# Order of the far stretches in the weighted value sums of a sliding-window attention kernel

## The chip, the core and the metric

The kernel runs on one core of a Trainium2 chip. A core has a matrix engine (TensorE, PE in the profile, with its weight loads shown apart as PEld), a vector engine (DVE), a scalar engine (ACT), GpSimd (POOL), a queue engine (SP) and 16 DMA engines. The metric is the device time of one execution in microseconds. Before the change the median of three runs is 258.38 us (258.15 to 258.97).

## The reference

The input is 2048 tokens of 512 channels. They are normalised, and the output is the sum of the input and of two branches.

- Branch A is attention with 32 heads of 16 channels. A token looks at itself and the 255 tokens before it. `qkv = xn @ wqkv`, `p = softmax(q k^T / 4)` inside the window, `o = p v`, and `o @ wo`.
- Branch B is a gated mixer: `z = gelu(xn @ w_in)` with 1376 channels; the second half is normalised and mixed over tokens by a full 2048 x 2048 matrix, a bias for each token is added, the product with the first half goes through `w_out`.

What the change touches is `o = p v` of branch A: for each block of queries, the sum of the value rows of at most 511 keys, weighted by the exponentials of the scores, and the sum of these weights.

## The kernel before

All work is in one program whose order is written out by hand in three strings of tokens, STAGE1, STAGE2 and STAGE3; each token is a call (the dictionary `ops`). An engine executes its instructions in the order of the tokens. STAGE1 computes branch B up to the gelu and the first projections; STAGE2 mixes tokens of branch B (`H`, line 553, matmuls of 344 columns), projects queries, keys and values (`Q`, `K`, `P`), and does the attention; STAGE3 ends with the last output projections. The tokens of attention lie between those of the mixing, so that TensorE has other work while the scalar engine takes exponentials.

Heads are taken in 4 groups G of 8. For one group:

- `S` (line 431) computes scores: keys on 128 partitions, queries along the columns, 8 heads, into the four banks of `sS`. `X` (line 445) takes the exponentials into `E`, a ring of 2560 columns for each of 8 heads. For a block of 128 keys, `kb`, `E` holds 320 columns of queries: partitions 0 to 63 hold the near keys, 64 to 127 the far ones, and the query columns of the two halves are shifted by 64, which is why a key block needs 320 columns and not 384. `M` multiplies the edges of the window by masks.
- `V` (`visit`, line 500) computes the value sums. There are 8 blocks u of 256 queries in a head group. For each, the sum runs over key blocks `2u-2` to `2u+1`, in two halves: half 0 (here called near) takes keys 0 to 63 of each key block, half 1 (far) takes keys 64 to 127. So a near matmul uses the rows 0 to 63 of the array, a far one rows 64 to 127. A weight load brings 64 keys x 17 columns of `v_all` (16 value channels and a column of ones, which makes the sum of the weights).
- A call `V,i` does the near half of block i and the far half of block i-1, one beside the other: the two write different banks (`oP`, two of them). The far half of block i-1 finishes that block, and `N` on the vector engine then reads the bank, divides, and transposes.

One stretch is a run of query columns that belongs to one key block and one half of the heads (`e`, 0 or 1). It is done by four pairs of weight load and matmul, one for each of 4 heads, in four strips of 32 output partitions (`32 * s`). A half of a full block has 8 stretches, two each of 64, 128, 192 and 256 columns, 1280 columns in all. A block at the start of a head group (u = 0) has only two key blocks: 4 stretches, of 128 and 256 columns in the near half and of 192 and 64 in the far half.

`av_half` (line 467) lists the stretches of one half in `todo`, sorts them by length, and yields each with `at`, the number of columns that this half has done before it. The near half goes from short to long, except for block u = 1, the far half from long to short. `visit` merges the two lists by `at`, so that the order of instructions follows the two halves as if each moved one column at the same time; with equal `at` the near one comes first. `V,32`, the last call, has a far half alone.

Of the kernel before, what the change touches and what calls it, by code (L numbers as in the profile page):

```python
# [31 lines left out]
BAND = 320  # L32
WARM = 29
NCEN = 3


def kb_start(kb):
    return BAND * kb if kb < NB - 1 else BAND * (NB - 2) + 256


def kb_len(kb):
    return min(BAND, S_TOK - kb * P)
# [135 lines left out]
def kernel(  # L178
# [69 lines left out]
    xs = s1.tile([P, NB, D], BF, name="xs")  # L248
    xc = s1.tile([P, NCEN, D], BF, name="xc")
    xcT = s1.tile([P, NCEN, NDC, P], BF, name="xcT")  # L250

# [30 lines left out]
    def x_transpose(n, bank):  # L282
        xn = xc[:, n, :] if n < NCEN else xs[:, n, :]
        tp = banks[bank].bitcast(BF)[:, 0:512].rearrange("p (c q) -> p c q", c=NDC)
        for c in range(NDC):
            nc.tensor.transpose(out=tp[:, c, :], in_=xn[:, c * P : (c + 1) * P], identity=ident[:])  # L286

    def x_copy(n, bank, eng):
        tp = banks[bank].bitcast(BF)[:, 0:512].rearrange("p (c q) -> p c q", c=NDC)
        if n < NCEN:  # L290
            for c in (0, 2):
# [14 lines left out]
    def gate(n, half, tag, p0, p1):  # L306
        zp = zrot[tag]
        f0 = half * FH
        for c in range(2 * p0, 2 * p1):
            for lo, hi in Z_RANGES:  # L310
                nc.tensor.matmul(  # L311
                    zp[:, lo:hi],
                    lhsT=xcT[:, n, c, :] if n < NCEN else xnT[:, c, n * P : (n + 1) * P],
                    rhs=w_in_sb[:, c, f0 + lo : f0 + hi],
# [4 lines left out]
    def gelu(n, half, tag):  # L319
        zp = zrot[tag]  # L320
        dst = z1u[:, n + 1, 0:FH] if half == 0 else z2[:, n, :]

        scale = rstdx[:, n : n + 1] if n < NCEN else 1.0
        nc.scalar.activation(out=dst, in_=zp[:, 0:FH], func=ACT.Gelu_apprx_tanh, scale=scale)  # L324
# [142 lines left out]
    def av_half(G, u, half):  # L467

        a = 2 * u
        r0 = 64 * half
        bank = oP[(G * 8 + u) % 2]
        todo = []
        for kb in range(max(0, a - 2), a + 2):

            lo = max(0, a * P - kb * P - r0)
            hi = min(kb_len(kb) - (r0 if kb >= NB - 2 else 0), (a + 2) * P - kb * P - r0)
            assert lo < hi, (u, half, kb)
            todo += [(hi - lo, kb, lo, hi, e) for e in range(2)]  # L480

        up = half == 0 and (G * 8 + u) % 8 != 1
        todo.sort(key=lambda t: (t[0] if up else -t[0], t[1], t[4]))
        at = 0
        for i, (n, kb, lo, hi, e) in enumerate(todo):
            o0 = e * 256 + kb * P + lo + r0 - a * P
            col = (kb_start(kb) + lo) % RING
            yield at, [
                dict(
                    out=bank[32 * s : 32 * s + DH + 1, o0 : o0 + n],  # L490
                    lhsT=v_all[r0 : r0 + 64, kb, HG * G + 4 * e + s, :],
                    rhs=E[r0 : r0 + 64, 4 * e + s, col : col + n],
                    start=(half == 0 and i == 0),
                    stop=(half == 1 and i == len(todo) - 1),
                )
                for s in range(4)
            ]
            at += n

    def visit(i):  # L500

        top = list(av_half(i // 8, i % 8, 0)) if i < NG * 8 else []
        low = list(av_half((i - 1) // 8, (i - 1) % 8, 1)) if i >= 1 else []
        if not top:

            nc.tensor.matmul(
                oP[i % 2][0 : DH + 1, 0:1], lhsT=v_all[0:64, 0, 0, :], rhs=E[0:64, 0, 0:1],
                start=True, stop=True, skip_group_check=True,
            )
        for _, four in sorted(top + low, key=lambda t: t[0]):  # L510
            for args in four:
                nc.tensor.matmul(skip_group_check=True, **args)  # L512
# [263 lines left out]
```

## Time and profile before

| | us |
|---|---|
| median of three runs | 258.38 |
| the profiled execution | 258.61 |
| its span, first to last instruction | 256.9 |
| around the span | 1.71 |
| TensorE busy | 248.8 |
| DVE busy | 186.2 |
| ACT busy | 181.0 |
| matmuls of the visits, line 512, busy | 24.8 |

The page gives each engine's busy time, a chain of the work that ended last, and groups of instructions by line with "busy, mean ns of one, idle before". A shape such as 64*17 64x256 says: 64 rows and 17 columns of weights, 256 columns of data. Matmuls overlap in the pipeline, and the profile's duration of one is its latency; how fast they follow one another is seen by counting starts in short windows. A row of such windows reads: window, its length, busy time of PE with the count of matmuls in it, busy time of PEld with the count of weight loads, the granted TensorE clock, the DMA share and GB/s. Windows that begin together and end later and later give running counts. The timeline merges neighbours of one kind: start, length, engine, line, names, shape of the first, count. The granted clock is 1.000 throughout.

### The profile page before, as it was taken

How to read it: one execution, taken by the hardware profiler on the slowest of the kernel's cores; microseconds unless marked ns; L12 is line 12 of the kernel's file. 1: busy time of each engine (PE TensorE's matmuls, PEld its weight loads, DVE VectorE, ACT ScalarE, POOL GpSimd, SP SyncE). 2: the span in 40 equal slices, each digit the busy share in tenths (PEclk: the TensorE clock that was granted, in tenths of full speed). 3: DMA queues.
4: the chain of work that ended last, by engine and by line, in shares of the span. 5: the costliest groups of instructions: out<-in, count | busy, mean ns of one | idle time of the engine just before them, and what ended most of it. 6: DMA issues, size and time to landing. Idle time of an engine off the chain costs nothing.

```text
span 256.9 us, 9051 instructions
## 1 busy us (share of the span) xinstructions
PE 248.8 (97%) x3900; PEld 139.3 (54%) x3936; DVE 186.2 (72%) x412; ACT 181.0 (70%) x142; POOL 92.0 (36%) x172
## 2 busy tenths in 40 slices
PE   7999999999999999999999999999999999999995
PEld 6565555433456555655555655655555544444454
DVE  4887877888797676768775767758877487666764
ACT  3686566899978687777778776867687787777400
POOL 7514110430016176017288053603645343611110
PEclk9999999999999999999999999999999999999999
DMA  7985743269404886659969549998775632644432
GB/s 233 362 242 103 124 82 81 72 134 220 100 3 86 111 148 137 116 110 133 145 125 166 115 83 113 128 148 146 140 144 114 125 74 84 115 123 119 115 98 68
DMA packets 69945, 32.67 MB, mean 127 GB/s; under 512 B 60833, under 2 KB 66945, under 8 KB 69905
## 3 DMA queue, kind: packets, MB, share of 16 engines
q1 hardware_dynamic: 64000, 20.79, 44.1%
q0 software_dynamic: 4672, 9.97, 17.6%
q10 hardware_dynamic: 1232, 1.32, 1.5%
q8 instruction: 31, 0.51, 0.9%
q14 instruction: 10, 0.07, 0.1%
HBM read 8.41 MB, written 2.10 MB: 41 GB/s over the span
## 4 chain that ended last, share of the span: by engine, by line
PE 93%; ACT 3%; issue 1%; DMA 1%; DVE 1%
PE w L553 31%; PE sS L431 10%; PE w L341 10%; PE oP L512 8%; PE w L583 6%; PE zb L311 5%; PE za L311 5%; PE zo L311 5%; PE w L396 4%; PE w L589 4%; ACT E L445 2%; DMA xs<-in_A_x_dram 1%; PE w L286 1%; PE w L605 1%; PE tj L583 1%
## 5 line engine op out<-in xcount | busy, mean ns | idle before, releaser
L445 ACT ACTIVATE E<-sS 128x2048 bf16<-128x2048 f32 x76 | 142.6, 1877 | 41.9 <-PE sS L431 40.8
L553 PE MATMUL w<-z,wspT 128*128 128x344 bf16 x512 | 92.6, 310 | 0.7 <-issue 0.2
L553 PEld LDWEIGHTS <-wspT 128*128 128x128 bf16 x512 | 46.9, 98 | 31.5 <-issue 5.9
L389 POOL DMA_DIRECT2D kbd<-kz x48 | 29.5, 623 | 60.4 <-DVE kz L381 58.3
L368 POOL DMA_DIRECT2D q<-qs x54 | 28.0, 529 | 29.2 <-DVE qs L357 22.0
L454 DVE TENSOR_TENSOR E<-E,mask 128x1024 bf16<-128x1024 bf16 x52 | 34.7, 675 | 4.3 <-ACT E L445 4.3
L341 PE MATMUL w<-xnT,wqkv 128*128 128x512 bf16 x106 | 35.7, 380 | 0.7 <-issue 0.3
L431 PE MATMUL sS<-q,kbd 32*128 32x320 bf16 (+4 forms) x816 | 30.4, 244 | 0.3
L560 DVE SCALAR_TENSOR_TENSOR z1u<-w,b_all,z1u 128x344 bf16<-128x344 f32 x32 | 18.2, 568 | 16.4 <-PE w L553 16.3
L520 DVE STREAM_TRANSPOSE a<-oP 128x512 f32<-128x512 f32 x32 | 22.7, 709 | 5.4 <-PE oP L512 5.3
L512 PE MATMUL oP<-E,v_all 64*17 64x256 bf16 (+3 forms) x1920 | 24.8, 230 | 0.4 <-issue 0.4
L512 PEld LDWEIGHTS <-v_all 64*17 64x17 bf16 x1920 | 20.2, 85 | 9.0 <-issue 8.8
L311 PEld LDWEIGHTS <-xnT 128*128 128x128 bf16 x208 | 18.3, 98 | 12.4
L431 PEld LDWEIGHTS <-kbd 32*128 32x128 bf16 x816 | 12.2, 92 | 22.2 <-issue 20.0
L583 PE MATMUL w<-w_out_sb,z1u 128*128 128x512 bf16 x67 | 19.1, 380 | 0.5 <-issue 0.3
L577 POOL DMA_DIRECT2D wqkv<-in_A_x_dram x16 | 8.9, 558 | 28.3 <-DVE out_sb L597 27.5
L341 PEld LDWEIGHTS <-wqkv 128*128 128x128 bf16 x128 | 12.1, 98 | 9.6 <-issue 1.2
L329 DVE BATCH_NORM_STATS2 st<-z 128x6 f32<-128x344 bf16 x32 | 14.4, 492 | 2.6 <-ACT z L324 2.6
L396 PE MATMUL w<-wqkv,xnT 128*128 128x512 bf16 x63 | 16.2, 380 | 0.0
L533 DVE STREAM_TRANSPOSE oT<-b 128x256 bf16<-128x256 bf16 x32 | 14.2, 445 | 1.1
L381 DVE CAST kz<-w 128x256 bf16<-128x256 f32 x26 | 9.8, 418 | 6.5 <-PE w L341 4.4
L589 PE MATMUL w<-wo_sb,oT 128*128 128x512 bf16 x47 | 13.8, 380 | 0.0
(95 smaller groups left out, 248.9 us busy)
## 6 DMA issues: line engine op xcount, KB each, us to landing
kbd<-kz POOLq DMA_DIRECT2D x48, 64.0 KB, 3.3
q<-qs POOLq DMA_DIRECT2D x36, 64.0 KB, 3.8
wqkv<-in_A_x_dram POOLq DMA_DIRECT2D x16, 128.0 KB, 3.5
wqkv<-in_A_wqkv_dram SPq DMA_DIRECT2D x1, 1536.0 KB
out_dram<-out_sb SPq DMA_DIRECT2D x11, 128.0 KB, 2.7
xs<-in_A_x_dram SPq DMA_DIRECT2D x2, 512.0 KB, 7.5
kbd<-kz SPq DMA_DIRECT2D x16, 64.0 KB, 2.1
q<-qs SPq DMA_DIRECT2D x14, 64.0 KB, 2.3
```

Source lines behind the costliest of these rows:

```text
L311: nc.tensor.matmul(zp[:, lo:hi], lhsT=xcT[:, n, c, :] if n < NCEN else xnT[:, c, n * P : (n + 1) * P], rhs=w_in_sb[:, c, f0 + lo : f0 + hi ...
L341: nc.tensor.matmul(banks[bank], lhsT=wqkv[:, c, col : col + P], rhs=xnT[:, c, tok : tok + 512], start=(c == 0), stop=(c == NDC - 1),)
L368: eng.dma_start(out=q2[h : P : 2, e, c : c + w], in_=t[64 * e : 64 * e + 64, src0 + at : src0 + at + w],)
L389: eng.dma_start(out=kbd[h : P : 2, slot : slot + 4, e, :], in_=t[64 * e : 64 * e + 64, h, :].rearrange("p (k m) -> p k m", k=4),)
L396: nc.tensor.matmul(banks[bank], lhsT=xnT[:, c, n * P : (n + 1) * P], rhs=wqkv[:, c, 2 * D : 3 * D], start=(c == 0), stop=(c == NDC - 1),)
L431: nc.tensor.matmul(s_bank(s)[:, off + o : off + o + w], lhsT=kbd[32 * s : 32 * s + 32, slot, ee, :], rhs=q2[32 * s : 32 * s + 32, ee, c : ...
L445: nc.scalar.activation(out=dst, in_=src, func=ACT.Exp, scale=SM_SCALE)
L454: nc.vector.tensor_tensor(out=reg, in0=reg, in1=mask[:].rearrange("p a m -> p (a m)").unsqueeze(1).to_broadcast([P, 8, 128]), op=ALU.mult,)
L512: nc.tensor.matmul(skip_group_check=True, **args)
L553: nc.tensor.matmul(banks[bank][:, 0:FQ], lhsT=w[:, c, :], rhs=z2[:, c, half * FQ : (half + 1) * FQ], start=(c == 0), stop=(c == NB - 1),)
L583: nc.tensor.matmul(banks[bank], lhsT=uT[:, c, :], rhs=w_out_sb[:, c, :], start=(c == 0), stop=False)
L589: nc.tensor.matmul(banks[bank], lhsT=oT[:, G, n * P : (n + 1) * P], rhs=wo_sb[:, G, :], start=False, stop=(G == NG - 1),)
```

## The change

The sorted list of the far half is put in another order by a fixed permutation. With lengths, the far half of a full block before and after:

- before: 256, 256, 192, 192, 128, 128, 64, 64 columns, so that stretches begin at columns 0, 256, 512, 704, 896, 1024, 1152, 1216
- FAR, blocks u = 1 to 6: 192, 128, 128, 64, 192, 256, 256, 64 columns, beginning at 0, 192, 320, 448, 512, 704, 960, 1216
- FAR_LAST, block u = 7, which lies beside the near half of the next head group's first block: 64, 128, 128, 256, 256, 192, 192, 64 columns, beginning at 0, 64, 192, 320, 576, 832, 1024, 1216

The near half of a full block begins its stretches at 0, 64, 128, 256, 384, 576, 768, 1024, and the first block of a head group at 0, 128, 256, 512. Block u = 0 keeps its order, as do all near halves. The stretch that ends the far half is the same as before. No instruction is added or taken away.

```diff
+FAR = (2, 4, 5, 6, 3, 0, 1, 7)
+FAR_LAST = (6, 4, 5, 0, 1, 2, 3, 7)
...
         up = half == 0 and (G * 8 + u) % 8 != 1
         todo.sort(key=lambda t: (t[0] if up else -t[0], t[1], t[4]))
+        if half == 1 and u:
+            todo = [todo[k] for k in (FAR_LAST if u == 7 else FAR)]
         at = 0
```

## The prediction

> **What bounds the kernel now.** I read the page first: the share of each engine, then the chain that ended last, then the groups of the changed line.
>
> ```profile
> span 256.9 us, 9051 instructions
> ...
> PE 248.8 (97%) x3900; PEld 139.3 (54%) x3936; DVE 186.2 (72%) x412; ACT 181.0 (70%) x142; POOL 92.0 (36%) x172
> ...
> PE 93%; ACT 3%; issue 1%; DMA 1%; DVE 1%
> PE w L553 31%; PE sS L431 10%; PE w L341 10%; PE oP L512 8%; PE w L583 6%; PE zb L311 5%; PE za L311 5%; PE zo L311 5%; PE w L396 4%; PE w L589 4%; ACT E L445 2%; DMA xs<-in_A_x_dram 1%; PE w L286 1%; PE w L605 1%; PE tj L583 1%
> ...
> L445 ACT ACTIVATE E<-sS 128x2048 bf16<-128x2048 f32 x76 | 142.6, 1877 | 41.9 <-PE sS L431 40.8
> ...
> L512 PE MATMUL oP<-E,v_all 64*17 64x256 bf16 (+3 forms) x1920 | 24.8, 230 | 0.4 <-issue 0.4
> L512 PEld LDWEIGHTS <-v_all 64*17 64x17 bf16 x1920 | 20.2, 85 | 9.0 <-issue 8.8
> ```
>
> TensorE is the bound: 97% busy, 93% of the chain, and the next engine, ACT, spends 40.8 of its 41.9 us of idle time there waiting for TensorE's scores. So what a visit (line 512) gains or loses reaches the end, unless TensorE meets a wait for something else soon after. All visits together are 8% of the chain, about 20 us, in 1920 pairs of a weight load and a matmul.
>
> The page cannot say how one visit runs, and its mean of 230 ns is latency, not spacing. So the second view is one ordinary full visit, at 118.38 us, with its matmuls kept apart by shape:
>
> ```profile
> L512 PE MATMUL oP<-E,v_all 64*17 64x256 bf16 x16 | 0.7, 271 | 0.0
> L512 PE MATMUL oP<-E,v_all 64*17 64x128 bf16 x16 | 0.6, 216 | 0.0
> L512 PE MATMUL oP<-E,v_all 64*17 64x64 bf16 x16 | 0.5, 191 | 0.0
> L512 PE MATMUL oP<-E,v_all 64*17 64x192 bf16 x16 | 0.4, 243 | 0.0
> ```
>
> From 64 to 256 columns is 80 ns more, so a column costs 0.417 ns and about 164 ns are pipeline latency. Sixty-four columns occupy their strip of the array for 27 ns, 128 for 53, 192 for 80, 256 for 107; I add 2 ns for the change.
>
> The third view opens windows that all begin with this visit and end later and later, for line 512 alone. The count behind PE is how many matmuls have started by the window's end, the count behind PEld how many weight loads:
>
> ```profile
> 118.38:118.43 0.05, 0.05 (x12) 0.05 (x15) 1.00 0.86 195
> 118.38:118.50 0.12, 0.12 (x16) 0.12 (x24) 1.00 1.12 216
> 118.38:118.53 0.15, 0.15 (x24) 0.15 (x32) 1.00 1.14 232
> 118.38:118.61 0.23, 0.23 (x28) 0.23 (x33) 1.00 1.17 246
> 118.38:118.62 0.24, 0.24 (x28) 0.24 (x35) 1.00 1.16 246
> 118.38:118.64 0.26, 0.26 (x32) 0.26 (x37) 1.00 1.43 248
> 118.38:118.70 0.32, 0.32 (x36) 0.32 (x37) 1.00 1.47 246
> 118.38:118.71 0.33, 0.33 (x38) 0.33 (x38) 1.00 1.46 246
> 118.38:118.79 0.41, 0.41 (x45) 0.41 (x48) 1.00 1.44 254
> 118.38:118.84 0.46, 0.46 (x48) 0.46 (x54) 1.00 1.79 311
> 118.38:118.87 0.49, 0.49 (x56) 0.49 (x57) 1.00 1.75 303
> 118.38:118.91 0.53, 0.53 (x58) 0.53 (x62) 1.00 1.66 289
> 118.38:118.94 0.56, 0.56 (x62) 0.56 (x64) 1.00 1.62 284
> 118.38:118.95 0.57, 0.57 (x64) 0.57 (x64) 1.00 1.60 279
> ```
>
> Three things stand in it. First, 15 loads go out in 0.05 us, one pair in 3.3 ns. Second, load 33 is out by 0.23 us at the latest, and then loads stop for reasons that are not in the code: 34 and 35 come between 0.23 and 0.24 us, load 37 by 0.26, load 38 only between 0.32 and 0.33. Third, from then on they come in steps: from x38 at 0.33 to x62 at 0.53 is 24 loads in 0.20 us, 8.3 ns each, though 15 went out in 0.05 us at the start.
>
> I read this as a limit on how many instructions may be unfinished. Thirty-two pairs are 64 instructions. The 65th and 66th go, and the 67th (load 34) goes about 0.03 us after the first matmul has ended (191 ns by its row). The 75th (load 38) goes just as much after the fifth matmul has ended: that is the first of the far half, 256 columns, started at about 14 ns, so done at 14 + 271 = 285 ns, and 285 + 35 = 320. So places come free in order, a matmul holds its place until it is finished, and a freed backlog is handed on at 4.2 ns an instruction.
>
> A shorter visit, in which the far half is that of a head group's first block and has only 4 stretches (96 instructions; the near half goes from long to short there), shows no such step:
>
> ```profile
> 112.05:112.25 0.20, 0.20 (x20) 0.20 (x28) 1.00 1.25 268
> 112.05:112.37 0.32, 0.32 (x32) 0.32 (x34) 1.00 1.12 238
> 112.05:112.38 0.33, 0.33 (x32) 0.33 (x36) 1.00 1.10 233
> ```
>
> The 65th instruction is due there only after places are free again, and two still go out within 0.01 us at 0.33 us.
>
> The Trainium skill, TensorE: Matmul & The Clock Gate, opening table of specifications, gives TensorE a queue of 64 with a partial reorder window; the stop after the 65th or 66th instruction agrees. It does not say that a place is held until the matmul ends; by the queue's depth alone, with places freed at issue, no stretch would be held up and the change would bring the small gain of the first rival below, so here the rows decide.
>
> **The change, part by part.** No instruction, wait, transfer or byte is added or removed, and on DVE, ACT, POOL, SP and the DMA queues nothing moves; their cost is nothing because no step of theirs is touched. Only the order of pairs inside 27 visits changes (and in the last, which has the far half alone): 24 full visits (6 in each head group) by FAR, and 3 at the change of head group by FAR_LAST. All far operands were complete when the near half of that block was visited before, so no wait is added; the last stretch is the same, so DVE's waiting transpose is released by the same matmul.
>
> What it removes: the shared columns, at 256 and 1024. At the first, matmuls 17 to 24 start between 0.12 and 0.15 us; the far one could start at 14 + 107 + 2 = 123 ns and had, by x24 at 0.15, at most some 10 ns of delay. At the second, matmuls 49 to 56 start between 0.46 and 0.49, where near was free at 0.349 + 0.109 = 0.458 (its eleventh group began with load 41, three steps of 8.3 ns after load 38, and 4 ns). I put each at 5 ns, bounds 0 and 10: 0 to 20 ns a visit.
>
> What it adds: it moves short far stretches forward and long ones back, so other work falls on places 65 and up. Groups of four pairs (one for each strip), N near, F far, with columns: before N64 F256 N64 N128 N128 F256 N192 F192, then N192 F192 N256 F128 N256 F128 F64 F64. After: N64 F192 N64 N128 F128 N128 F128 N192, then F64 F192 N192 F256 N256 F256 N256 F64. Before, the ninth group was not due until about 0.26 and the tenth not until 0.32, when the place was free anyway. After, the far half runs at 14, 96, 151 ns and its 64 columns are due at 206 ns, the next F192 at 235 ns. In ns, first and fourth strip:
> - ninth, F64: 206, and by loads 34 to 36 at 230 and more, 247 for the fourth.
> - tenth, F192: load 37 at 253, matmul 257. The fifth matmul is now 192 columns, done 271 - 243 = 28 ns earlier, so load 38 goes at 320 - 28 = 292: strips two to four at 296, 304, 313. They were due at 240 to 270.
> - eleventh, N192, due at 259: pairs 8.3 ns apart, so 321 to 346.
> - twelfth, F256: first strip 354, the others behind the tenth's 80 + 2 ns: 378, 386, 395.
> - thirteenth, N256: 403 to 428. Fourteenth, F256: 463 to 504. Fifteenth, N256: 403 + 109 = 512 to 537. Sixteenth, F64: 463 + 109 = 572, and 596 to 613.
>
> The last matmul starts at 613 ns instead of about 566 (x62 at 0.56, x64 at 0.57): 47 later. The near half's last column leaves at 537 + 107 = 644 instead of about 485 + 107 = 592: 52 later. I take 49 ns for a full visit. Bounds: if the tenth group were let go only at 0.32, as now, 28 ns more, 77; if neither half were ever held, the near half alone would be 1280 columns, 533 + 7 x 2 + 10 = 557 ns against 592, a gain of 35. I take 49 because it uses the two delays that the rows show, unchanged.
>
> The visits with 4 near stretches at the change of head group have 96 instructions; the far half's first eight groups are done early and nothing is due before its place is free. They lose up to 20 ns of sharing: 0.01 us each, 0.03 together. The last visit has 32 pairs and no near half: nothing.
>
> What of 24 x 49 reaches the end is seen in what follows a visit:
>
> ```profile
> 73.14 0.76 PE L512 MATMUL oP<-E,v_all 64*17 64x64 bf16 x64
> 73.99 0.40 PE L431 MATMUL sS<-q,kbd 32*128 32x320 bf16 x8
> ...
> 118.38 0.76 PE L512 MATMUL oP<-E,v_all 64*17 64x64 bf16 x64
> 119.07 0.40 PE L431 MATMUL sS<-q,kbd 32*128 32x192 bf16 x8
> ...
> 191.92 0.76 PE L512 MATMUL oP<-E,v_all 64*17 64x64 bf16 x64
> 192.66 0.40 PE L431 MATMUL sS<-q,kbd 32*128 32x320 bf16 x8
> ```
>
> The ordinary visit hands over after 0.69 us; the visit at 73.14 only after 0.85 and the one at 191.92 after 0.74, because the scores behind them wait for ACT to free the banks. There 0.05 us each is hidden. Sum: 24 x 0.049 = 1.18, less 2 x 0.05 and less 0.03: **+1.05 us**. The profiled execution took 258.61 us, 1.71 around its span of 256.9; that makes 259.66 for it. It stands 0.23 above the median of the runs, 258.38, so for the median I say **259.4 us**, 0.4% slower.
>
> **The rivals.**
> First, the small gain. The two halves share no row of the array, and if a load can only hide behind the other half's matmuls, a common change leaves both idle; taken apart, nothing idles. For it: the far half did start late at column 256. Against it: at most 20 ns a visit are there to win, 24 x 0.010 to 0.020 = 0.24 to 0.48 us, so 257.9 to 258.1; over 0.3% (0.78 us, about what a measurement of this kernel can tell from no change) needs the whole 35 ns of the bound, 24 x 35 = 0.84, 257.5. It decides if load 38 comes no later than the work it feeds is due. The Trainium skill, same page, Part 3, The mechanism, has this rule: loads overlap matmuls in flight only where the row groups differ. In this trace loads 17 to 24 are out by x24 at 0.12 us, while matmuls of both halves are in flight, so the rule as written isn't what the rows show.
> Second, the loss is there but soaked up: TensorE meets more waits for ACT than the two I counted, as a later TensorE shortens them. For it: ACT is 70% busy. Against: its idle time is nearly all waiting for TensorE. With half soaked up, +0.5, 258.9.
> Third, the block is worse: tied to 0.32 us whatever the first far stretch is. 24 x 77 = 1.85, less the hidden 0.15: 260.1. Against it: load 34 follows the first matmul's end by the same 0.03.
> That the change did not do what it says is no case: the far half's columns 192, 320, 448, 512, 704, 960, 1216 meet none of 64, 128, 256, 384, 576, 768, 1024; at the head group's change 64, 192, 320, 576, 832, 1024, 1216 meet none of 128, 256, 512.
>
> **How the numbers follow.** Forecast (35 to 60 ns a visit, 258.38 + 0.75 to 1.35, so 259.1 to 259.7): 0.66. Third rival: 0.09. Second: 0.12. First: 0.13, of which 0.05 pass the bound. The forecast's lower edge touches 0.3%, so I give slower 0.73, same 0.22, faster 0.05. The range leaves out the far parts of the first and third: 258.0 to 260.1.
>
> **What would show it.** In a full visit of the new kernel load 38 should come by about 0.29 to 0.30 us, 16 matmuls behind it 8.3 ns apart, the last matmul at 0.61, and the hand-over at 0.73 to 0.74 instead of 0.69; the 96-instruction visits should be alike or 0.01 shorter; other lines alike. If the hand-over is at 0.67, the limit is not held until a matmul ends, and the forecast is wrong; if visits are longer but the span is not, the second rival is right.

## The result and the profile after

The changed kernel takes 259.97 us in the median (259.07 to 260.45, six runs) against 258.34 us before (six runs, the three of the opening among them). The ratio is estimated from all runs at 1.0057, a little under that of the two medians, with a 95% interval of 1.0036 to 1.0077, that is 0.9 to 2.0 us slower. The profiled execution took 259.57 us, with a span of 257.9 us where the kernel before had 256.9.

The page of the changed kernel (all lines of the code below the change have moved by 4 or 6, so visits are line 518 here):

```profile
span 257.9 us, 9087 instructions
...
PE 252.7 (98%) x3936; PEld 138.4 (54%) x3936; DVE 186.4 (72%) x412; ACT 181.0 (70%) x142; POOL 92.0 (36%) x172
...
PE 95%; ACT 2%; DMA 1%; DVE 1%; issue 0%
...
L518 PE MATMUL oP<-E,v_all 64*17 64x128 bf16 (+3 forms) x1920 | 26.1, 230 | 0.2 <-issue 0.2
```

TensorE is still the bound. The same 1920 matmuls of the visits, each with the same mean of 230 ns, now cover 26.1 us instead of 24.8: they follow one another more slowly, by 1.3 us in all. (The sum of TensorE's busy time is not compared: the trace before lacks 36 matmuls of other lines, x3900 against x3936.)

The same full visit as in the prediction, at 118.66 us here, in windows for line 518 that begin with it; counts of started matmuls behind PE, of started loads behind PEld:

```profile
118.66:118.81 0.15, 0.15 (x24) 0.15 (x32) 1.00 1.33 265
118.66:118.88 0.22, 0.22 (x32) 0.22 (x33) 1.00 1.48 258
118.66:118.89 0.23, 0.23 (x33) 0.23 (x33) 1.00 1.46 257
118.66:118.90 0.24, 0.24 (x34) 0.24 (x35) 1.00 1.45 257
118.66:118.95 0.29, 0.29 (x36) 0.29 (x37) 1.00 1.53 277
118.66:118.96 0.30, 0.30 (x37) 0.30 (x38) 1.00 1.85 327
118.66:119.17 0.51, 0.51 (x55) 0.51 (x63) 1.00 1.48 262
118.66:119.24 0.58, 0.58 (x60) 0.58 (x64) 1.00 1.39 257
118.66:119.28 0.62, 0.62 (x63) 0.60 (x64) 1.00 1.32 247
118.66:119.29 0.63, 0.63 (x64) 0.60 (x64) 1.00 1.30 243
```

The first 32 loads are out by 0.15 us, as before. Loads 34 and 35 come at 0.23 to 0.24, as before. Load 38 comes at 0.29 to 0.30 instead of 0.32 to 0.33, and 25 loads follow in 0.21 us, 8.4 ns each. The last matmul starts at 0.62 instead of 0.57. At 0.51 already 63 loads are out and 55 matmuls have started: the loads are no longer what the end waits for, the delayed stretches are. The timeline shows the hand-over to the next work, for this visit, for the two whose successors wait for ACT, and for one of 96 instructions:

```profile
73.15 0.81 PE L518 MATMUL oP<-E,v_all 64*17 64x64 bf16 x64
74.01 0.40 PE L435 MATMUL sS<-q,kbd 32*128 32x320 bf16 x8
...
106.19 0.74 PE L518 MATMUL oP<-E,v_all 64*17 64x128 bf16 x48
106.89 0.42 PE L435 MATMUL sS<-q,kbd 32*128 32x64 bf16 x12
...
118.66 0.81 PE L518 MATMUL oP<-E,v_all 64*17 64x64 bf16 x64
119.41 0.40 PE L435 MATMUL sS<-q,kbd 32*128 32x192 bf16 x8
...
192.55 0.81 PE L518 MATMUL oP<-E,v_all 64*17 64x64 bf16 x64
193.30 0.40 PE L435 MATMUL sS<-q,kbd 32*128 32x320 bf16 x8
```

The ordinary visit hands over after 0.74 to 0.75 us, against 0.69. The two with a wait behind them took 0.85 and 0.74 before and take 0.86 and 0.75 now: there the loss is hidden. The visit of 96 instructions takes 0.70 us, as it did in the kernel before:

```profile
105.92 0.74 PE L512 MATMUL oP<-E,v_all 64*17 64x128 bf16 x48
106.62 0.41 PE L431 MATMUL sS<-q,kbd 32*128 32x64 bf16 x12
```

### The profile page after: what moved, and what is told of

Its sections match the earlier page's. It is cut to its first block, busy times and chain, and to the rows that moved or that the text cites. A ratio compares the mean times of both kernels' runs of the same rounds, so it can differ in the third digit from the quotient of the medians.

```text
span 257.9 us, 9087 instructions
## 1 busy us (share of the span) xinstructions
PE 252.7 (98%) x3936; PEld 138.4 (54%) x3936; DVE 186.4 (72%) x412; ACT 181.0 (70%) x142; POOL 92.0 (36%) x172
## 4 chain that ended last, share of the span: by engine, by line
PE 95%; ACT 2%; DMA 1%; DVE 1%; issue 0%
PE w L559 31%; PE w L345 11%; PE sS L435 10%; PE oP L518 9%; PE w L589 6%; PE w L400 5%; PE za L315 5%; PE zb L315 5%; PE zo L315 5%; PE w L595 4%; ACT E L449 1%; DMA xs<-in_A_x_dram 1%; PE w L290 1%; PE ti L589 1%; PE w L611 1%; PE tj L589 1%
## 5 line engine op out<-in xcount | busy, mean ns | idle before, releaser
L345 PE MATMUL w<-xnT,wqkv 128*128 128x512 bf16 x128 | 41.1, 380 | 0.0
L518 PE MATMUL oP<-E,v_all 64*17 64x128 bf16 (+3 forms) x1920 | 26.1, 230 | 0.2 <-issue 0.2
L518 PEld LDWEIGHTS <-v_all 64*17 64x17 bf16 x1920 | 19.3, 85 | 8.8 <-issue 8.5
```

The lines of the kernel that those rows point to most:

```text
L345: nc.tensor.matmul(banks[bank], lhsT=wqkv[:, c, col : col + P], rhs=xnT[:, c, tok : tok + 512], start=(c == 0), stop=(c == NDC - 1),)
```

## The experiments

The reordering raises one question above all: does the order cost because of which stretches run beside each other, or because of where the 64th instruction falls? All experiments start from the kernel before and change the order inside a visit, the number of strips, or both.

**Long far stretches early, still no shared column.**

```diff
         todo.sort(key=lambda t: (t[0] if up else -t[0], t[1], t[4]))
+        if half == 1 and 1 <= u <= 6:
+            want = (192, 256, 256, 192, 64, 128, 128, 64)
+            todo = [todo.pop([t[0] for t in todo].index(w)) for w in want]
```

> Far order 192, 256, 256, 192, 64, 128, 128, 64 in blocks u = 1 to 6 (u = 7 as before): no shared column, like the change, but the long stretches early, so that the ninth and tenth groups of four pairs are not due before 0.25 and 0.31 us of a visit. Theory of the limit on unfinished instructions: load 38 at 0.29 to 0.30 us because the first far stretch is 192 columns, nothing held up, hand-over at 0.67 to 0.68 us instead of 0.69 (before) and 0.74 (the change), whole kernel 0.3 to 0.5 us faster than before. Rival, that leaving the shared columns is itself what costs: hand-over near 0.74, about 1.3 us slower.

Windows of one full visit (line 515 there; it begins at 118.13, so 0.01 us after the windows), and its hand-over in the timeline:

```profile
118.12:118.36 0.24, 0.23 (x32) 0.23 (x34) 1.00 1.69 269
118.12:118.42 0.30, 0.29 (x36) 0.29 (x37) 1.00 1.63 272
118.12:118.43 0.31, 0.30 (x36) 0.30 (x38) 1.00 1.69 285
118.12:118.69 0.57, 0.56 (x64) 0.56 (x64) 1.00 1.48 254
```

```profile
118.13 0.74 PE L515 MATMUL oP<-E,v_all 64*17 64x64 bf16 x64
118.80 0.40 PE L431 MATMUL sS<-q,kbd 32*128 32x192 bf16 x8
```

Load 38 comes at 0.29 to 0.30 us, as in the changed kernel, for the first far stretch has 192 columns in both. But here nothing is due before it, and the visit hands over after 0.67 us. So the separation of columns is not what costs. The gain of 0.3 to 0.5 us that was expected for the whole is not seen: 258.49 us against 258.53, ratio 1.000 (0.9982 to 1.0017). Some 0.015 us in 24 visits, 0.36 us, would be 0.14%. In this profile at least six of the 24 visits hand over no earlier than before, though their last matmul starts earlier (the one at 77.96 us after 0.70, for example), which leaves at most 0.27 us. Either figure lies inside the interval, so how much reaches the end is not settled.

**All seven columns shared.**

```diff
+        if (half == 1 and 1 <= u <= 6) or (half == 0 and u >= 2):
+            want = (64, 256, 192, 128, 256, 192, 128, 64)
+            todo = [todo.pop([t[0] for t in todo].index(w)) for w in want]
```

> Both halves of a full visit take the same order, 64, 256, 192, 128, 256, 192, 128, 64, so that all seven changes of stretch share a column. Limit on unfinished instructions: the first matmuls are short and free their places early, the ninth group is not due before 0.27 us, so hand-over at 0.67 to 0.69 us, the same as before or up to 0.4 us faster. Rival, that a shared column leaves both halves idle at the load: seven of them at the 7 to 10 ns seen in the kernel before, or more, hand-over at 0.72 us or later, 0.7 us or more slower than before.

The visit (line 515, it begins at 118.19):

```profile
118.19:118.42 0.23, 0.23 (x25) 0.23 (x33) 1.00 1.85 265
118.19:118.46 0.27, 0.27 (x32) 0.27 (x39) 1.00 1.71 257
118.19:118.75 0.56, 0.56 (x64) 0.56 (x64) 1.00 1.59 240
```

```profile
118.19 0.74 PE L515 MATMUL oP<-E,v_all 64*17 64x64 bf16 x64
118.86 0.40 PE L431 MATMUL sS<-q,kbd 32*128 32x192 bf16 x8
```

With every change of stretch on a common column the visit is as short as the best, 0.67 us. The fifth matmul has 64 columns here and ends early, and load 38 does not stop at all: 39 loads are out by 0.27 us. The whole kernel takes 258.35 us, ratio 0.9991 (0.9977 to 1.0005): no slower, and no gain that can be told from none. A shared column is no cost that these runs can show.

**The two parts of the change apart.** First FAR alone, then FAR_LAST alone:

```diff
+        if half == 1 and 1 <= u <= 6:
+            todo = [todo[k] for k in (2, 4, 5, 6, 3, 0, 1, 7)]
```

> The change without FAR_LAST: only the 24 full visits are reordered. Limit on unfinished instructions: the whole loss stays, hand-over of full visits 0.74, time as the changed kernel (1.0 to 1.6 us slower than before). If FAR_LAST carried a part, the time would be between.

```diff
+        if half == 1 and u == 7:
+            todo = [todo[k] for k in (6, 4, 5, 0, 1, 2, 3, 7)]
```

> Only FAR_LAST, the three visits of 96 instructions at a change of head group and the last visit. Limit theory and its rivals: hand-over of these visits 0.69 to 0.70 as before, time within 0.1 us of before.

FAR alone: 259.93 us, ratio 1.0052 (1.0032 to 1.0072). FAR_LAST alone: 258.41 us, ratio 0.9995 (0.9982 to 1.0008). The full visit, from the timelines of FAR alone and of FAR_LAST alone:

```profile
119.32 0.81 PE L514 MATMUL oP<-E,v_all 64*17 64x64 bf16 x64
120.06 0.40 PE L431 MATMUL sS<-q,kbd 32*128 32x192 bf16 x8
```

```profile
118.29 0.75 PE L514 MATMUL oP<-E,v_all 64*17 64x64 bf16 x64
118.98 0.40 PE L431 MATMUL sS<-q,kbd 32*128 32x192 bf16 x8
```

0.74 us and 0.69 us. No loss is seen without FAR, and with FAR alone it is as large as with both.

**Fewer instructions over the same columns.** Without its fourth strip a full visit has 96 instructions instead of 128, and every stretch keeps its place and length. Such a kernel leaves out the value sums of one head in four; the two banks are preset to 1 instead of 0, so that the sums of weights that nobody writes are not divided by as zeros. The order of before and that of the change, both so (the second has the lines of the change besides):

```diff
-                for s in range(4)
+                for s in range(3)
...
-            nc.vector.memset(t[:], 0.0)
+            nc.vector.memset(t[:], 1.0)
```

> The order of the kernel before, with the fourth strip of every stretch left out (one head in four has no value sum), so that a full visit has 96 instructions over the same columns. Limit on unfinished instructions: the 65th instruction lies in the eleventh group, due long after the first places are free, so no stop of the loads near 0.18 to 0.23 us and hand-over at 0.66 to 0.68 us.

> The order of the change (FAR and FAR_LAST), with the fourth strip of every stretch left out as in its companion. Limit on unfinished instructions: the loss goes with the instructions, hand-over within 0.015 us of the companion's, whole time within 0.4 us of it. Rival, that the order itself costs (where the halves change, which banks and strips run side by side): columns and changes are all still there, so about 0.05 us a visit and 1.1 to 1.3 us in all stay between the two.

The visit in the order of before, then in that of the change:

```profile
119.22 0.74 PE L512 MATMUL oP<-E,v_all 64*17 64x64 bf16 x48
119.89 0.40 PE L431 MATMUL sS<-q,kbd 32*128 32x192 bf16 x8
```

```profile
118.16 0.73 PE L514 MATMUL oP<-E,v_all 64*17 64x64 bf16 x48
118.82 0.40 PE L431 MATMUL sS<-q,kbd 32*128 32x192 bf16 x8
```

Both hand over after 0.66 to 0.67 us, and the kernels take 257.68 us (257.52 to 258.66) and 257.53 us (257.47 to 257.78): ratios to the kernel before of 0.9952 (0.9934 to 0.9971) and 0.9950 (0.9934 to 0.9967). With a quarter of the visits' instructions gone the change costs nothing that can be seen, though in the three strips left all its columns and neighbours are there. The order costs only together with the number of instructions. (Both kernels are 1.1 to 1.3 us faster than the kernel before, 258.82 us beside them. Visits that are 0.02 us shorter make 0.5 of that; no visit in their profiles has the pause of the last section; whether that is the rest is not shown.)

**A long matmul in the first place.**

```diff
+        if half == 0 and u >= 2:
+            want = (256, 64, 64, 128, 128, 192, 192, 256)
+            todo = [todo.pop([t[0] for t in todo].index(w)) for w in want]
```

> The near half of a full visit begins with one of its 256-column stretches, then 64, 64, 128, 128, 192, 192, 256; the far half as before. If a place is freed when the matmul that holds it has ended, the first matmul ends 80 ns later than in the kernel before, and load 34 comes at about 0.31 us instead of 0.23, hand-over at 0.72 to 0.73. If load 34 waits for a fixed time or for the supply of instructions, it stays at 0.23 us.

Windows of a full visit (line 515, it begins at 119.19, 0.01 us after the windows), and its hand-over:

```profile
119.18:119.42 0.24, 0.23 (x26) 0.23 (x33) 1.00 1.11 255
119.18:119.48 0.30, 0.29 (x32) 0.29 (x33) 1.00 1.31 258
119.18:119.49 0.31, 0.30 (x33) 0.30 (x33) 1.00 1.30 257
119.18:119.50 0.32, 0.31 (x34) 0.32 (x34) 1.00 1.30 258
119.18:119.80 0.62, 0.61 (x64) 0.61 (x64) 1.00 1.42 265
```

```profile
119.19 0.80 PE L515 MATMUL oP<-E,v_all 64*17 64x256 bf16 x64
119.91 0.40 PE L431 MATMUL sS<-q,kbd 32*128 32x192 bf16 x8
```

Load 33 is out by 0.23 us, and load 34 comes only at 0.30 to 0.31 us: 0.08 later than with 64 columns first, just as much as the first matmul lasts longer (271 against 191 ns by the rows in the prediction). Matmul 33, the 66th instruction, comes just ahead of it in the same 0.01 us. The hand-over is at 0.72 us. So the stop is tied to the end of the first matmul by its row, and not to a time; nor would a supply of instructions at its own pace move with that matmul's length. The kernel was run once (259.76 us), which is too little to judge its whole time.

## Why the prediction was right

The forecast was 259.4 us and slower; measured 259.97. That is inside the range that was given, to 260.1, but above the forecast's own 259.1 to 259.7, and by the time alone nearer to the third rival's 260.1. What decides between the two is not the time but the visit: the rival's 77 ns would put the hand-over at 0.77 us and load 38 at 0.32. Point by point:

- **TensorE is the bound, and a visit's loss passes through.** Right: the visits' matmuls cover 1.3 us more, and the whole is slower by a like amount.
- **A place is held until its matmul ends, places come free in order, and the backlog moves at 8.3 ns a pair.** Right, and now shown from three sides: load 34 moves with the length of the first matmul (0.23 to 0.31 us); load 38 follows that of the fifth (0.32 us for 256 columns, 0.29 to 0.30 for 192, no stop for 64); with 96 instructions the loss is gone. One reading was wrong: "the 65th and 66th go". Only the 65th, load 33, goes (at 161 ns in the changed kernel, before the first matmul's end at 191). The 66th, matmul 33, waits for the first matmul's end like load 34: it starts just ahead of load 34 at 0.22 to 0.23 us in the changed kernel (32 matmuls by 0.22, 33 by 0.23, 34 loads only after that) and at 0.30 behind a first matmul of 256 columns. The rows of before could not show this, for there matmul 33 wasn't due until 0.26 us.
- **Load 38 at 0.29 to 0.30, last matmul at 0.61, hand-over at 0.73 to 0.74.** Measured 0.29 to 0.30, 0.62, 0.74 to 0.75.
- **49 ns a visit** was somewhat small. The line's busy time gives 1.3 us in 24 visits, some 54 ns, and the hand-over moves from 0.69 to 0.74 or 0.75. Two matmuls were let go too early: the ninth group's first at 206 ns, when it waits until 0.22 to 0.23 us, and the tenth group's first at 257 ns with load 37, when the rows have x36 matmuls still at 0.29 us and x37 only with load 38 at 0.30. So the far chain of the first strip ran later than worked out: its last matmul, the 61st, was to start at 572 ns, and only 60 have started by 0.58 us. But a visit ends with its fourth strip, and there the sum was 6 ns short: the last matmul at 613 ns, measured 619 by the trace. Of that, 3 ns are load 38 (295 against 292) and 3 are the matmuls of 192 columns behind it, whose successors start 85 ns after them where 82 was taken; why 85 the runs don't show.
- **The shared columns are worth 0 to 20 ns a visit.** Nothing says that they cost more, and even that looks generous: with seven of them a visit is as short as in the best order with none.
- **Two visits hide the loss.** Right, both (0.85 to 0.86, 0.74 to 0.75). **0.03 us from the visits at a change of head group:** not seen; 0.70 us in both.
- **The sum**, +1.05 us: 24 visits at 54 ns less the two that hide it make 1.2 us, and the interval is 0.9 to 2.0. The single profiles differ by 1.0, the medians by 1.63; the mechanism's 1.2 lies inside the interval, and the runs give no reason to look for a second cause. They don't exclude one of a few tenths of a microsecond either.

The first rival is refuted by the change itself, which has no shared column in a full visit and is slower, and by the kernel in which all seven are shared and the visit takes 0.67 us. The first experiment alone would fit it: without shared columns its visit is 0.02 us shorter, which is what that rival promised. The Trainium skill's rule behind it (TensorE: Matmul & The Clock Gate, Part 3, The mechanism: loads overlap matmuls in flight only where the row groups differ) doesn't hold as a cost here: with both halves changing weights together seven times the visit took 0.67 us. The third, a stop fixed at 0.32 us, falls by the row at 0.30. The second, a loss that ACT's waits soak up, is refuted for the loss. The gain of 0.015 us a visit that two of the orders bring could not be told from none in the whole time.

## What to carry to other kernels

Many short weight loads and matmuls can be limited not by the array but by how many of them may be unfinished: here some 32 pairs, 64 instructions, given back in order some 0.03 us after the oldest matmul ends by the profile. Loads and matmuls alternate in every kernel here, so the runs don't tell whether pairs or instructions are counted. In such a run, put a short matmul first and long stretches early, so that the work behind the 64th instruction isn't due before places are free, or use fewer pairs; where two independent halves change their weights mattered little here. A count of starts in windows of 10 ns showed the stop and its pace from one trace, where mean durations (230 ns in both kernels) showed nothing; that it hangs on the oldest matmul took the experiments.

## What was unexpected in the hardware

The freed places are handed on at 4.2 ns an instruction, 8.3 or 8.4 ns a pair, slower than TensorE takes them at the start of a visit (15 loads in 0.05 us). Once work is due that still waits for a place, it comes at this pace even when every operand is there, and in the changed kernel the visit stays behind to its end.

One visit has a pause of another kind, behind its 50th load in both kernels, and of a different length in different profiles. Windows of line 512 in the kernel before:

```profile
124.36:124.85 0.49, 0.49 (x50) 0.49 (x50) 1.00 0.06 8
124.36:125.50 1.14, 0.74 (x50) 0.51 (x50) 1.00 0.08 21
124.36:125.51 1.15, 0.74 (x50) 0.51 (x51) 1.00 0.08 22
124.36:125.54 1.18, 0.77 (x56) 0.54 (x59) 1.00 0.09 23
```

Nothing starts for some 0.65 us, and then nine loads go out within 0.04 us: the 8.3 ns pace is gone, as it would be if all places were free by then. The same visit in the kernel before, in the changed kernel and with FAR alone, from the timelines:

```profile
124.36 0.74 PE L512 MATMUL oP<-E,v_all 64*17 64x64 bf16 x50
125.51 0.30 PE L512 MATMUL oP<-E,v_all 64*17 64x256 bf16 x14 [0.41 <-issue]
```

```profile
124.70 0.69 PE L518 MATMUL oP<-E,v_all 64*17 64x64 bf16 x50
125.63 0.39 PE L518 MATMUL oP<-E,v_all 64*17 64x256 bf16 x14 [0.24 <-issue]
```

```profile
125.35 0.81 PE L514 MATMUL oP<-E,v_all 64*17 64x64 bf16 x64
126.10 1.05 PE L555 MATMUL w<-z,wspT 128*128 128x344 bf16 x6
```

It is shorter in the changed kernel (0.24 us idle against 0.41; the pipeline's latency covers the rest) and absent with FAR alone. It isn't the only one: the changed kernel also stops for 0.14 us behind the 62nd load of its visit at 174.67 us (62 loads by 0.51 us, the 63rd by 0.64), the kernel with a long matmul first has them in other visits (at 95.58 and 178.36 us), and the two kernels of three strips show none: all their full visits start the last matmul at 0.54 to 0.55 us. The profile puts the pause down to "issue", that is, to nothing that it shows. The instructions may have been supplied late, but no run here tested that. It moves a single profile by tenths of a microsecond, which is a reason to judge a change of this size by several runs and by the visits themselves.
